# Left keys and values loaded with 16 positions outermost, and the last block's routing given in two parts

## The chip, the cores and the metric

The kernel runs on one core of a Trainium2 chip. The metric is the time of one launch on the device in microseconds; the time before is the median of three runs. The engines are TensorE (PE in the profile; its weight loads are PEld), VectorE (DVE), ScalarE (ACT), GpSimd (POOL) and SyncE (SP), which issues nearly all DMA transfers here.

## The reference

Three layers follow each other, all in float32.

```python
# attention: q, k, v are (8 batches, 8 heads, 576 positions, 64)
k_p = k.reshape(B, H, 72, 8, D).mean(axis=3)      # pooled keys: 72 per head
v_p = v.reshape(B, H, 72, 8, D).mean(axis=3)
attn = softmax(q @ k_p^T / 8)                      # with 1e-9 in the denominator
x = (attn @ v_p) -> (4608 tokens, 512)
# dense layer: w_in (512, 2048), w_out (2048, 512)
x = softplus(x @ w_in) @ w_out
# mixture of 8 experts: w1 (8, 512, 1024), w2 (8, 1024, 512)
logits = normalised(x) @ normalised(expert_emb)^T / tau
e = argmax(logits);  gate = softmax(logits)[e]
out = gate * (relu(x @ w1[e]) @ w2[e])
```

## The kernel before, in words

**Stages.** Tokens go in 12 blocks of 384 (`NB`). While TensorE computes the dense layer of one block (`mm1`, `mm2`, 16 feature chunks each), the attention of later tokens is worked in between, by a plan of gaps (`make_plan`). Each float32 product is made of three matmuls of split operands (`three`, lines 641 to 643), so every operand has a rounded part and a remainder: ScalarE copies the first, VectorE or GpSimd subtracts for the second. After a block's dense layer, `x2_out` splits its result and stores it to `x2s` in DRAM. `split_ss`, `logits_x`, `logits_s` and `route` then find the expert and the gate of each token. After the tenth block `pick` takes the most frequent expert so far; its weights are loaded and split (`load_a`, `make_a`, `load_w2`) during the last block, and behind it all tokens go through that expert in nine pairs of 512 tokens with a Strassen scheme: seven products (`mm3s`) and then `mm4s`. `load_b` fetches a pair's tokens, `make_t` forms four sums on GpSimd (eight instructions, line 923 to 934), `split_t` splits them on ScalarE and VectorE (942, 943) into the tile `T`, of which there is one buffer. `work_list` makes a list of the blocks that have tokens of other experts, which a loop at the end works off.

**Pooled keys and values.** For one batch the keys are 576 rows of 2 KB: 4 pairs of heads (`NJ`), and 144 pooled rows in a pair (`PK`), each row with its eight positions side by side. Of each pair 128 rows go the main way (`fetch_main`) and 16 are left (`LEFT`). `fetch_kl` loads the 64 left key rows into 64 partitions, pair by pair; `fetch_vl` loads the left value rows of two pairs into 32 partitions, three times over (rounded part, the same again, remainder), and this for two groups. `prep_k` and `prep_r` sum the eight positions, `kT` transposes the keys and puts the left columns behind the 128 of each pair, `build_r` masks the left values with `lm`, so that a matmul with `RV` picks a pair out of its group, `spread` copies the left weights of the attention three times side by side (line 364), `atrans` transposes them into `aR`, and `av` multiplies.

**What sets the order.** TensorE and SyncE work in the order in which the program calls them. For the first block the order of all engines is written out by hand (`ORDER`: a capital letter is a step of a generator, a small letter a load, H an idle matmul). After that a scheduler orders VectorE, ScalarE and GpSimd by the times of a simulation; an instruction given to `keep_in_program_order` is queued behind the instruction that its engine had been given last before it. The steps that follow a block's dense layer are put into a list, `front`, and one entry is taken per gap; in the part with the pairs `fronts(n)` takes n entries at fixed places:

```python
for p in range(1, NPR):
    run(split_t(p))
    fronts(2)
    if p + 1 < NPR:
        load_b(p + 1)
        run(make_t(p + 1))
    both(mm3s(p, 0), mm4s(p - 1, 1))
    fronts(1)
    both(mm3s(p, 1), mm4s(p, 0))
```

In the last block `make_t(0)` is taken step by step at chunks 4 to 11 and `split_t(0)` at chunks 12 to 15.

Of the kernel before, what the change touches and what calls it, by code (L numbers as in the profile page):

```python
# [20 lines left out]
def tile_attention_moe_moe(  # L21
# [77 lines left out]
    def setup_consts():  # L99
# [12 lines left out]
        nc.vector.tensor_scalar(pb, pi, LEFT, None, ALU.bitwise_and)  # L112
# [114 lines left out]
    def fetch_kl(b):  # L227
        st = stp.tile([P, POOL * D], F32, tag="st", name="st")
        nc.sync.dma_start(st[0:64, :], rows(k, b).rearrange("(j r) c -> j r c", j=NJ)[:, P:PK, :])
        st_t["kl", b] = st  # L230

    def fetch_vl(b, g):
        if b < 2:
            st = stp.tile([P, POOL * D], F32, tag="st", name="st")
        else:
            if g == 0:
                st_t["vl2", b] = stp.tile([P, 2, POOL * D], F32, tag="st", name="st")
            st = st_t["vl2", b][:, g, :]
        src = rows(v, b).rearrange("(j r) c -> j r c", j=NJ)[2 * g:2 * g + 2, P:PK, :]
        for i in range(3):  # L240
            nc.sync.dma_start(st[32 * i:32 * (i + 1), :], src)
        st_t["vl", b, g] = st
# [15 lines left out]
    def kT(b):  # L258
# [12 lines left out]
        copy(kb[:, :, P:PK], pk2.rearrange("p (j l) -> p j l", j=NJ))  # L271
# [28 lines left out]
    def build_r(b):  # L300
        vl = kv_t.pop(("l", b))
        vlm = kp.tile([96, NJ, D], F32, tag="vlm", name=f"vlm{b}")
        for jj in range(2):
            part = vlm.rearrange("p (g j) d -> p g j d", j=2)[:, :, jj, :]
            times(part, vl, lm[0:96, jj:jj + 1], b, "A" if alt(f"U{b}.m{jj}") else "G")
            yield
        nc.scalar.copy(RV[0:96, :, 1, :], vlm)
        yield
        nc.vector.tensor_tensor(RV[64:96, :, 1, :], vlm[64:96], f32(RV)[64:96, :, 1, :], ALU.subtract)
        yield  # L310
# [46 lines left out]
    def spread(t):  # L357
        e = e_t[t]
        el = qp.tile([P, 2, 3, 2, LEFT], F32, tag="el", name=f"el{t}")
        el_t[t] = el  # L360
        ev = e.rearrange("p (j h) k -> p j h k", h=2)
        for g in range(2):
            copy = nc.scalar.copy if alt(f"E{t}.e{g}") else nc.vector.tensor_copy
            copy(el[:, g], ev[:, 2 * g:2 * g + 2, 1, SP - LEFT:].unsqueeze(1).to_broadcast([P, 3, 2, LEFT]))
            yield
# [28 lines left out]
    def atrans(t):  # L394
# [8 lines left out]
        for g in range(2):  # L403
            nc.tensor.transpose(pl[:, g, :], el[:, g].rearrange("p r j l -> p (r j l)"), ident)
# [12 lines left out]
    def av(si, j):  # L417
# [9 lines left out]
        nc.tensor.matmul(pv[:, 0:n], rv, aR[:, j // 2, kk], start=False, stop=False)  # L427
# [95 lines left out]
    def emit_step(o):  # L523
# [14 lines left out]
        elif o[0] == "FV":  # L538
            for i in range(2):
                fetch_v(o[1], i)  # L540
            for i in range(2):
                fetch_vl(o[1], i)
# [195 lines left out]
    def route(blk):  # L738
# [8 lines left out]
        nc.gpsimd.tensor_tensor(n, lt[:, :, 2 * E], half, ALU.pow)  # L747
        nc.vector.tensor_scalar(n, n, 1e-6, taut, ALU.add, ALU.mult)
# [188 lines left out]
    def split_t(p):  # L937
# [3 lines left out]
        for i in (2, 0, 3, 1):  # L941
            nc.scalar.copy(t[:, 0, i], bf[:, i])
            nc.vector.tensor_tensor(t[:, 1, i], bf[:, i], f32(t)[:, 0, i], ALU.subtract)
# [180 lines left out]
    def loads(c, *a):  # L1124
# [10 lines left out]
        k0.0 k0.1 l0 q0 v0.0 q1 v0.1 i0 q2 r0.0 o0 l1 i1 H H H H H H H H H H H H K0 K0 H H H H H H H H K0 K0  # L1135
        H H K0 r0.1 Q0 K0 K0 H q3 H i2 Q0 B0 B0 H H B0 H V0 B0 V0 S0 S0 S0 Q1 S0 H q4 H S0 k1.0 Q1 H o1 o3 H
        k1.1 i3 H v1.1 v1.0 H i4 H o2 S0 V0 S1 V0 S0 S1 S1 S0 I0 W0 S1 S0 W0 S1 I0 S0 I0 Q2 S0 S1 W0 H H H
        I0 H H Q2 H H H H W0 E0 T0 I0 E0 S2 R0 S1 T0 T0 S2 S2 S1 I0 H H H H H O0 H S2 H I0 H H S1 S2 O0 O0
        I1 S2 O0 I1 R0 S2 I1 T0 T0 S2 Q3 O0 I1 H q5 H o4 Q3 H H H H S2 T0 H H H U0 U0 S2 S3 I2 i6 S1 o5 r1.0
        I2 I2 S3 S2 S3 U0 H I2 H H H H Q4 U0 S1 T2 E2 I2 Q4 E2 I2 I1 S3 T1 E1 E1 S3 T2 T2 S3 T1 I2 T1 T2 O1  # L1140
        T1 T1 K1 O1 O1 T1 S3 O1 T2 O3 O3 S3 O1 I1 T2 S3 O3 X2 I1 K1 O3 I3 X0 I3 I3 K1 O3 X2 I3 X1 X0 X2 K1
        X0 X3 - X1 K1 M0 X3 X1 r1.1 V1 i7 K1 X3 K1 M0 S3 I4 S3 M0 I4 M0 V1 I4 O2 B1 E3 E3 I4 B1 M1 G0 O2 B1
# [50 lines left out]
    with tc.block(schedule_with_timeline_sim=True), tc.manual_schedule(engines={mybir.EngineType.PE, mybir.EngineType.SP}):  # L1193
# [17 lines left out]
        def run_mm2(blk, fc):  # L1211
            run(mm2(blk, fc))
            if fc == NFC - 1:
# [6 lines left out]
                front.append(lambda: route(blk))  # L1220
                if blk == NB - 1:
# [113 lines left out]
```

## Time and profile before

| | |
|---|---|
| median of three runs | 1414.24 us (1412.03 to 1416.3) |
| profiled execution | 1414.68 us, span 1412.9 us |
| TensorE busy | 1364.6 us, 97% of the span, 8126 matmuls |
| VectorE busy | 901.1 us, 64% |
| ScalarE busy | 774.3 us, 55% |
| GpSimd busy | 419.5 us, 30% |
| granted TensorE clock | 0.988 of full speed in the mean |
| DMA | 100.00 MB, mean 71 GB/s |
| chain that ended last | PE 87%, DVE 6%, DMA 2%, ACT 2%, POOL 2%, issue 1% |

Busy time is time in which an instruction of the engine ran. An instruction of VectorE that waits for a memory port counts as running. The chain is followed back from the last instruction to what released each one. In a timeline, brackets behind an instruction give the idle time of its engine before it and what ended this.

### The profile page before, as it was taken

The page shows a single profiled execution, that of the slowest core. Times are in us where ns is not written, and L with a number is a line of the kernel's source. Part 1 is how long each engine was busy: PE and PEld are TensorE (multiplying, and loading weights), DVE is VectorE, ACT ScalarE, POOL GpSimd, SP SyncE. Part 2 cuts the span into 40 slices and gives each one's busy share as a digit, 9 for nine tenths or more (in the row PEclk, how much of TensorE's full clock was granted, in tenths as well). Part 3 has the DMA queues.
Part 4 walks back from the last instruction along what each step waited for, and adds up shares of the span by engine and source line. Part 5 has one row for each costly group of instructions (what it writes and reads, how often), then busy time and mean ns, then how long its engine had stood idle before and what let it go on. Part 6 is the DMA issues. An engine that isn't in the chain of part 4 may idle for free.

```text
span 1412.9 us, 21410 instructions
## 1 busy us (share of the span) xinstructions
PE 1364.6 (97%) x8126; PEld 1281.5 (91%) x8126; DVE 901.1 (64%) x1858; ACT 774.3 (55%) x1697; POOL 419.5 (30%) x374
## 2 busy tenths in 40 slices
PE   6789999999999999999999999999999999999998
PEld 5567889999999999999999999998988989989987
DVE  6989677677677676767676655567556444445332
ACT  4676656566676666667666767567632222223221
POOL 5843232223132231313223222164261222221200
PEclk8899999999999999999999999999999999999999
DMA  7562421212021210302120101042051302222000
GB/s 225 168 217 78 130 60 43 67 49 85 24 87 38 68 53 1 101 9 86 50 60 9 53 1 46 0 146 64 16 164 53 124 26 69 90 90 90 30 31 31
DMA packets 97881, 100.00 MB, mean 71 GB/s; under 512 B 40424, under 2 KB 79336, under 8 KB 97776
## 3 DMA queue, kind: packets, MB, share of 16 engines
q1 hardware_dynamic: 97776, 98.60, 22.5%
q8 instruction: 66, 1.08, 0.3%
q14 instruction: 39, 0.32, 0.1%
HBM read 70.27 MB, written 28.31 MB: 70 GB/s over the span
## 4 chain that ended last, share of the span: by engine, by line
PE 87%; DVE 6%; DMA 2%; ACT 2%; POOL 2%; issue 1%; SPq 0%; POOLq 0%; DVEq 0%; ACTq 0%
PE h L641 9%; PE h L643 9%; PE h L642 9%; PE acc L641 8%; PE acc L642 8%; PE acc L643 8%; PE y L641 4%; PE y L642 4%; PE y L643 4%; PE m L641 4%; PE m L642 4%; PE m L643 4%; PE pp L333 2%; PE acc L689 2%; DMA q<-in_q_dram 1%; PE lg L721 1%
## 5 line engine op out<-in xcount | busy, mean ns | idle before, releaser
L641 PE MATMUL h<-xT,wi 128*128 128x384 f32 x768 | 265.3, 345 | 3.6 <-DVE t L669 1.4
L642 PE MATMUL h<-xT,wi 128*128 128x384 f32 x768 | 257.9, 336 | 2.5 <-DVE xT L442 2.5
L643 PE MATMUL h<-xT,wi 128*128 128x384 f32 x768 | 258.3, 336 | 0.0
L641 PE MATMUL acc<-g,wo 128*128 128x384 f32 x704 | 241.0, 342 | 0.7 <-POOL wo L632 0.7
L642 PE MATMUL acc<-g,wo 128*128 128x384 f32 x704 | 236.4, 336 | 2.4 <-DVE g L673 2.4
L643 PE MATMUL acc<-g,wo 128*128 128x384 f32 x704 | 236.6, 336 | 0.0
L632 POOL TENSOR_TENSOR wo<-wof,wo 128x512 fp32r<-128x512 f32 x80 | 104.8, 1310 | 392.2 <-ACT wo L628 392.2
L657 ACT ACTIVATE t<-h 128x384 f32<-128x384 f32 x192 | 94.0, 490 | 154.0 <-PE h L643 152.5
L673 DVE TENSOR_TENSOR g<-t,g 128x384 fp32r<-128x384 f32 x176 | 142.2, 811 | 46.1 <-ACT g L671 46.1
L669 DVE SCALAR_TENSOR_TENSOR t<-h,t 128x384 f32<-128x384 f32 x176 | 97.0, 553 | 90.9 <-ACT t L661 88.9
L641 PEld LDWEIGHTS h<-xT,wi 128*128 128x128 f32 x768 | 145.0, 189 | 6.8 <-DVE t L669 2.0
L628 ACT CAST wo<-wof 128x512 fp32r<-128x512 f32 x176 | 109.3, 621 | 75.0 <-PE acc L643 73.5
L642 PEld LDWEIGHTS h<-xT,wi 128*128 128x128 f32 x768 | 144.8, 189 | 4.5 <-DVE xT L442 3.3
L643 PEld LDWEIGHTS h<-xT,wi 128*128 128x128 f32 x768 | 144.6, 188 | 0.0
L642 PEld LDWEIGHTS acc<-g,wo 128*128 128x128 f32 x704 | 132.9, 189 | 2.7 <-DVE g L673 2.7
L641 PEld LDWEIGHTS acc<-g,wo 128*128 128x128 f32 x704 | 132.7, 188 | 2.3 <-POOL wo L632 1.0
L643 PEld LDWEIGHTS acc<-g,wo 128*128 128x128 f32 x704 | 132.5, 188 | 0.0
L641 PE MATMUL y<-w2h,g 128*128 128x512 f32 x288 | 112.9, 392 | 0.0
L642 PE MATMUL y<-w2l,g 128*128 128x512 f32 x288 | 112.9, 392 | 0.0
L643 PE MATMUL y<-w2h,g 128*128 128x512 f32 x288 | 112.8, 392 | 0.0
L671 ACT CAST g<-t 128x384 fp32r<-128x384 f32 x176 | 89.6, 513 | 24.8 <-DVE t L669 24.0
L661 ACT ACTIVATE t<-t 128x384 f32<-128x384 f32 x192 | 100.7, 527 | 4.0
(223 smaller groups left out, 2856.4 us busy)
## 6 DMA issues: line engine op xcount, KB each, us to landing
x2s<-x SPq DMA_DIRECT2D x12, 1536.0 KB
b<-x2s SPq DMA_DIRECT2D x27, 512.0 KB
out_dram<-o SPq DMA_DIRECT2D x36, 256.0 KB
st<-in_k_dram SPq DMA_DIRECT2D x16, 512.0 KB
q<-in_q_dram SPq DMA_DIRECT2D x32, 256.0 KB
st<-in_v_dram SPq DMA_DIRECT2D x16, 512.0 KB
st<-in_moe_w_in_dram SPq DMA_DIRECT2D x16, 512.0 KB
st<-in_moe_w_out_dram SPq DMA_DIRECT2D x16, 512.0 KB
```

What stands on the lines that cost most here:

```text
L333: nc.tensor.matmul(pp[p0:p0 + n, i, :], qT[:, j, p0:p0 + n], kbd_t[b][:, j, :], start=True, stop=True)
L628: nc.scalar.copy(w[:, 0, :], wof[fc])
L632: eng.tensor_tensor(w[:, 1, :], wof[fc], f32(w)[:, 0, :], ALU.subtract)
L641: nc.tensor.matmul(ps, ll, rh, start=first, stop=False, skip_group_check=more)
L642: nc.tensor.matmul(ps, lh, rl, start=False, stop=False, skip_group_check=more)
L643: nc.tensor.matmul(ps, lh, rh, start=False, stop=last, skip_group_check=more)
L657: nc.scalar.activation(t, h, AF.Abs)
L661: nc.scalar.activation(t, t, AF.Ln, bias=1.0)
L669: nc.vector.scalar_tensor_tensor(t, h, 0.0, t, ALU.max, ALU.add)
L671: nc.scalar.copy(g[:, 0, :], t)
L673: nc.vector.tensor_tensor(g[:, 1, :], t, f32(g)[:, 0, :], ALU.subtract)
L689: nc.tensor.matmul(accs[blk][d], wof[fc][:, dd], f32(g)[:, 0, :], start=(fc == 0), stop=(fc == NFC - 1))
```

## The change

The left rows are loaded with the 16 positions outermost and the pairs inside, for keys and for values. All that depends on the order of the left rows follows: the columns of the transposed left keys, the mask `lm` (now by the lowest bit of the partition's number), the order in `spread`'s copies and the transposes, and which half of `aR` a pair uses. The left values of all four pairs come in one load per copy, three instead of six, into one tile; in `ORDER` the loads r0 and r1 stand for both groups, where r0.0 and r1.0 stood.

`route` gives control back after the power on GpSimd. For the last block alone it is taken in two parts, one entry of `front` later than before and the second part another entry later, with `work_list` behind it. In `split_t` both instructions of each split are kept in program order for the first pair.

```diff
--- before.py
+++ after.py
@@ -109,7 +109,7 @@
         nc.vector.tensor_scalar(hm[:, 0:1], pf, float(SP), None, ALU.is_lt)
         nc.vector.tensor_scalar(hm[:, 1:2], pf, float(SP), None, ALU.is_ge)
         pb = cp.tile([P, 1], I32, name="pb")
-        nc.vector.tensor_scalar(pb, pi, LEFT, None, ALU.bitwise_and)
+        nc.vector.tensor_scalar(pb, pi, 1, None, ALU.bitwise_and)
         nc.vector.tensor_copy(pf, pb)
         nc.vector.tensor_scalar(lm[:, 0:1], pf, 0.5, None, ALU.is_lt)
         nc.vector.tensor_scalar(lm[:, 1:2], pf, 0.5, None, ALU.is_ge)
@@ -226,20 +226,18 @@
 
     def fetch_kl(b):
         st = stp.tile([P, POOL * D], F32, tag="st", name="st")
-        nc.sync.dma_start(st[0:64, :], rows(k, b).rearrange("(j r) c -> j r c", j=NJ)[:, P:PK, :])
+        nc.sync.dma_start(st[0:64, :], rows(k, b).rearrange("(j r) c -> r j c", j=NJ)[P:PK])
         st_t["kl", b] = st
 
-    def fetch_vl(b, g):
-        if b < 2:
-            st = stp.tile([P, POOL * D], F32, tag="st", name="st")
-        else:
-            if g == 0:
-                st_t["vl2", b] = stp.tile([P, 2, POOL * D], F32, tag="st", name="st")
-            st = st_t["vl2", b][:, g, :]
-        src = rows(v, b).rearrange("(j r) c -> j r c", j=NJ)[2 * g:2 * g + 2, P:PK, :]
+
+
+    def fetch_vl(b):
+        st = stp.tile([P, 2, POOL * D], F32, tag="st", name="st")
+        src = rows(v, b).rearrange("(j r) c -> r j c", j=NJ)[P:PK]
         for i in range(3):
-            nc.sync.dma_start(st[32 * i:32 * (i + 1), :], src)
-        st_t["vl", b, g] = st
+            nc.sync.dma_start(st[32 * i:32 * (i + 1)], src)
+        for g in range(2):
+            st_t["vl", b, g] = st[:, g, :]
 
 
     def prep_k(b):
@@ -268,7 +266,7 @@
         (nc.scalar.copy if alt(f"B{b}.c1") else nc.vector.tensor_copy)(kb[:, :, 0:P], pk)
         yield
         copy = nc.scalar.copy if alt(f"B{b}.c2") else nc.vector.tensor_copy
-        copy(kb[:, :, P:PK], pk2.rearrange("p (j l) -> p j l", j=NJ))
+        copy(kb[:, :, P:PK], pk2.rearrange("p (l j) -> p j l", j=NJ))
         kbd_t[b] = kb
         yield
 
@@ -301,7 +299,7 @@
         vl = kv_t.pop(("l", b))
         vlm = kp.tile([96, NJ, D], F32, tag="vlm", name=f"vlm{b}")
         for jj in range(2):
-            part = vlm.rearrange("p (g j) d -> p g j d", j=2)[:, :, jj, :]
+            part = vlm.rearrange("p (j g) d -> p g j d", g=2)[:, :, jj, :]
             times(part, vl, lm[0:96, jj:jj + 1], b, "A" if alt(f"U{b}.m{jj}") else "G")
             yield
         nc.scalar.copy(RV[0:96, :, 1, :], vlm)
@@ -356,12 +354,12 @@
 
     def spread(t):
         e = e_t[t]
-        el = qp.tile([P, 2, 3, 2, LEFT], F32, tag="el", name=f"el{t}")
+        el = qp.tile([P, 2, 3, LEFT, 2], F32, tag="el", name=f"el{t}")
         el_t[t] = el
-        ev = e.rearrange("p (j h) k -> p j h k", h=2)
+        ev = e.rearrange("p (j g h) k -> p g h k j", g=2, h=2)
         for g in range(2):
             copy = nc.scalar.copy if alt(f"E{t}.e{g}") else nc.vector.tensor_copy
-            copy(el[:, g], ev[:, 2 * g:2 * g + 2, 1, SP - LEFT:].unsqueeze(1).to_broadcast([P, 3, 2, LEFT]))
+            copy(el[:, g], ev[:, g, 1, SP - LEFT:, :].unsqueeze(1).to_broadcast([P, 3, LEFT, 2]))
             yield
 
 
@@ -401,7 +399,7 @@
         e_t.pop(t)
         pl = ps_tile([96, 2, P], "pl")
         for g in range(2):
-            nc.tensor.transpose(pl[:, g, :], el[:, g].rearrange("p r j l -> p (r j l)"), ident)
+            nc.tensor.transpose(pl[:, g, :], el[:, g].rearrange("p r l j -> p (r l j)"), ident)
         yield
         for c0, d0, n in col_pieces(t):
             dd, cc = slice(d0, d0 + n), slice(c0, c0 + n)
@@ -424,7 +422,7 @@
         kk = slice(k0, k0 + n)
         nc.tensor.matmul(pv[:, 0:n], vl, aH[:, j, kk], start=True, stop=False)
         nc.tensor.matmul(pv[:, 0:n], vh, aL[:, j, kk], start=False, stop=False)
-        nc.tensor.matmul(pv[:, 0:n], rv, aR[:, j // 2, kk], start=False, stop=False)
+        nc.tensor.matmul(pv[:, 0:n], rv, aR[:, j % 2, kk], start=False, stop=False)
         nc.tensor.matmul(pv[:, 0:n], vh, aH[:, j, kk], start=False, stop=True)
         yield
         for c0, t0, m in pieces:
@@ -538,8 +536,7 @@
         elif o[0] == "FV":
             for i in range(2):
                 fetch_v(o[1], i)
-            for i in range(2):
-                fetch_vl(o[1], i)
+            fetch_vl(o[1])
         elif o[0] in ("PK", "KT", "PV", "PR"):
             if o not in preps:
                 preps[o] = {"PK": prep_k, "KT": kT, "PV": prep_v, "PR": prep_r}[o[0]](o[1])
@@ -745,6 +742,7 @@
         ts = slice(blk * TPB, (blk + 1) * TPB)
         n = sm.tile([P, TPB], F32, tag="n", name="n")
         nc.gpsimd.tensor_tensor(n, lt[:, :, 2 * E], half, ALU.pow)
+        yield
         nc.vector.tensor_scalar(n, n, 1e-6, taut, ALU.add, ALU.mult)
         nc.vector.reciprocal(n, n)
         z = sm.tile([P, TPB, E], F32, tag="z", name="z")
@@ -939,8 +937,12 @@
         t = p2[0].tile([P, 2, 4, 2, HT], F32R, tag="T", name=f"T{p}")
         t_t[p] = t
         for i in (2, 0, 3, 1):
-            nc.scalar.copy(t[:, 0, i], bf[:, i])
-            nc.vector.tensor_tensor(t[:, 1, i], bf[:, i], f32(t)[:, 0, i], ALU.subtract)
+            both_ins = [nc.scalar.copy(t[:, 0, i], bf[:, i])]
+            both_ins.append(nc.vector.tensor_tensor(t[:, 1, i], bf[:, i], f32(t)[:, 0, i], ALU.subtract))
+
+            if p == 0:
+                for ins in both_ins:
+                    tc.keep_in_program_order(ins)
             yield
 
     HOMES = ["g", "g", "g", "st", "W", "W", "wo", "wo"]
@@ -1132,14 +1134,14 @@
     }
 
     ORDER = """
-        k0.0 k0.1 l0 q0 v0.0 q1 v0.1 i0 q2 r0.0 o0 l1 i1 H H H H H H H H H H H H K0 K0 H H H H H H H H K0 K0
-        H H K0 r0.1 Q0 K0 K0 H q3 H i2 Q0 B0 B0 H H B0 H V0 B0 V0 S0 S0 S0 Q1 S0 H q4 H S0 k1.0 Q1 H o1 o3 H
+        k0.0 k0.1 l0 q0 v0.0 q1 v0.1 i0 q2 r0 o0 l1 i1 H H H H H H H H H H H H K0 K0 H H H H H H H H K0 K0
+        H H K0 Q0 K0 K0 H q3 H i2 Q0 B0 B0 H H B0 H V0 B0 V0 S0 S0 S0 Q1 S0 H q4 H S0 k1.0 Q1 H o1 o3 H
         k1.1 i3 H v1.1 v1.0 H i4 H o2 S0 V0 S1 V0 S0 S1 S1 S0 I0 W0 S1 S0 W0 S1 I0 S0 I0 Q2 S0 S1 W0 H H H
         I0 H H Q2 H H H H W0 E0 T0 I0 E0 S2 R0 S1 T0 T0 S2 S2 S1 I0 H H H H H O0 H S2 H I0 H H S1 S2 O0 O0
-        I1 S2 O0 I1 R0 S2 I1 T0 T0 S2 Q3 O0 I1 H q5 H o4 Q3 H H H H S2 T0 H H H U0 U0 S2 S3 I2 i6 S1 o5 r1.0
+        I1 S2 O0 I1 R0 S2 I1 T0 T0 S2 Q3 O0 I1 H q5 H o4 Q3 H H H H S2 T0 H H H U0 U0 S2 S3 I2 i6 S1 o5 r1
         I2 I2 S3 S2 S3 U0 H I2 H H H H Q4 U0 S1 T2 E2 I2 Q4 E2 I2 I1 S3 T1 E1 E1 S3 T2 T2 S3 T1 I2 T1 T2 O1
         T1 T1 K1 O1 O1 T1 S3 O1 T2 O3 O3 S3 O1 I1 T2 S3 O3 X2 I1 K1 O3 I3 X0 I3 I3 K1 O3 X2 I3 X1 X0 X2 K1
-        X0 X3 - X1 K1 M0 X3 X1 r1.1 V1 i7 K1 X3 K1 M0 S3 I4 S3 M0 I4 M0 V1 I4 O2 B1 E3 E3 I4 B1 M1 G0 O2 B1
+        X0 X3 - X1 K1 M0 X3 X1 V1 i7 K1 X3 K1 M0 S3 I4 S3 M0 I4 M0 V1 I4 O2 B1 E3 E3 I4 B1 M1 G0 O2 B1
         I4 G0 O2 B1 G0 O2 I3 T3 I4 G0 T3 G1 P0 O4 O2 O4 O4 O4 I6 P0 G1 I3 I4 G1 M2 I6 I6 O4 G1 O5 O5 O5 Z2
         I6 T3 I3 O5 P1 Z4 R1 G2 Z2 O5 o6 G2 P1 Z4 G2 o7 i5 q6 i9 i8 R1 I7 T3 M3 I7 G2 T3 I7 G2 T3 V1 o8 U1
         G2 U1 I7 M4 G3 O6 O6 O6 V1 I6 G3 O6 G3 P2 O7 O7 O7 I7 O6 G4 P2 I6 O7 I5 G4 G3 I5 S4 O7 G4 I5 Z6 S4
@@ -1217,8 +1219,13 @@
                 front.extend([lambda: None] * WAIT2)
                 front.append(lambda: [logits_x(blk, d) for d in range(KC)] + [logits_s(blk)])
                 front.append(lambda: None)
-                front.append(lambda: route(blk))
-                if blk == NB - 1:
+                r = route(blk)
+                if blk < NB - 1:
+                    front.append(lambda: run(r))
+                else:
+                    front.append(lambda: None)
+                    front.append(lambda: next(r))
+                    front.append(lambda: run(r))
                     front.append(work_list)
                 if blk == NB - 3:
                     front.append(count)
```

## Rows read from the trace of the kernel before

**Rows 1.** Stages of the run: length, busy time of each engine, granted clock, DMA share, GB/s.
```profile
0.00:110.00 110.00, 81.19 (x397) 65.40 (x398) 93.77 (x162) 66.89 (x132) 63.33 (x81) 0.88 0.64 196
110.00:300.00 190.00, 185.93 (x1075) 171.34 (x1075) 141.96 (x296) 120.29 (x266) 53.90 (x46) 1.00 0.26 74
300.00:900.00 600.00, 600.00 (x3624) 588.47 (x3623) 405.01 (x831) 398.72 (x875) 163.79 (x142) 1.00 0.16 47
...
1100.00:1380.00 280.00, 280.00 (x1759) 253.41 (x1759) 127.16 (x291) 77.62 (x186) 60.15 (x46) 1.00 0.19 65
```

**Rows 2.** Timeline of SyncE's DMA queue: start, time to issue, instruction (count).
```profile
14.78 4.55 SPq L241 DMA_DIRECT2D st<-in_v_dram  x3
19.43 0.53 SPq L173 DMA_DIRECT2D q<-in_q_dram  x1
```

**Rows 3.** Stages again: the first 10 us, and 22 to 24 us.
```profile
0.00:10.00 10.00, 5.54 (x29) 5.31 (x30) 4.22 (x14) 2.23 (x4) 4.81 (x19) 0.97 0.89 235
...
22.00:24.00 2.00, 0.04 (x1) 0.00 (x0) 2.00 (x5) 1.41 (x3) 1.29 (x1) 1.00 0.14 49
```

**Rows 4.** Timeline, 28 to 40 us: start, duration, instruction, [idle before it <- releaser].
```profile
29.67 1.08 PE L316 MATMUL pq<-ident,q 128*128 128x128 f32 x4 [7.62 <-DMA q<-in_q_dram]
...
28.98 0.72 POOL L193 TENSOR_TENSOR st<-st 96x256 f32<-96x256 f32 x1 [5.44 <-DMA st<-in_v_dram]
...
31.01 1.14 DVE L591 TENSOR_SCALAR st<-st 128x512 int32<-128x512 int32 x1 [2.63 <-DMA st<-in_moe_w_in_dram]
...
30.79 0.59 ACT L319 COPY qT<-pq 128x512 f32<-128x512 f32 x1 [4.43 <-PE pq L316]
...
32.60 1.14 POOL L353 TENSOR_TENSOR e<-e,sm 128x576 f32<-128x576 f32 x1
33.71 1.27 POOL L632 TENSOR_TENSOR wo<-wof,wo 128x512 fp32r<-128x512 f32 x1
34.94 1.15 POOL L353 TENSOR_TENSOR e<-e,sm 128x576 f32<-128x576 f32 x1
36.05 1.29 POOL L598 TENSOR_TENSOR st<-st,wi 128x512 f32<-128x512 f32 x1
...
33.91 3.97 DVE L593 SCALAR_TENSOR_TENSOR st<-st 128x512 int32<-128x512 int32 x1
...
39.13 0.25 DVE L364 COPY el<-e 128x96 f32<-128x96 f32 x1
```

**Rows 5.** Tile `st`, 0 to 130 us: durations in ns (min/median/max), first and last start.
```profile
L593 DVE SCALAR_TENSOR_TENSOR st<-st x16: 677/742/3970, 18.4 to 128.3; 128x512 int32<-128x512 int32 x16
```

**Rows 6.** Timeline, 957 to 963 us, VectorE and TensorE.
```profile
957.39 2.48 DVE L943 TENSOR_TENSOR T<-bf,T 128x512 fp32r<-128x512 f32 x4
...
962.08 0.69 PE L642 MATMUL acc<-g,wo 128*128 128x384 f32 x1 [2.45 <-DVE g L673]
```

**Rows 7.** Stages again: 960 to 970 us.
```profile
960.00:970.00 10.00, 7.92 (x38) 7.93 (x39) 5.90 (x8) 6.09 (x14) 6.99 (x5) 0.83 0.17 52
```

**Rows 8.** Timeline, 1052 to 1065 us, TensorE's waits and one of VectorE.
```profile
1052.20 0.37 PE L742 MATMUL pt<-ident,l 32*128 32x32 f32 x3 [1.12 <-ACT l L735]
...
1061.46 0.39 PE L641 MATMUL m<-T,a 128*128 128x256 f32 x1 [2.15 <-DVE c L1009]
...
1064.57 0.39 PE L641 MATMUL m<-T,a 128*128 128x256 f32 x1 [1.42 <-DVE c L994]
...
1058.48 1.24 DVE L748 TENSOR_SCALAR n<-n,taut 128x3 f32<-128x3 f32 x1 [1.19 <-POOL n L747]
```

**Rows 9.** Timeline, 1088 to 1136 us: SyncE's queue, GpSimd, VectorE.
```profile
1088.31 0.33 SPq L1083 DMA_DIRECT2D lst<-ebi  x1
...
1097.06 1.29 POOL L923 TENSOR_TENSOR bf<-bz 128x512 f32<-128x512 f32 x1 [33.25 <-DMA bz<-x2s]
...
1090.96 2.49 DVE L943 TENSOR_TENSOR T<-bf,T 128x512 fp32r<-128x512 f32 x4
...
1133.30 2.49 DVE L943 TENSOR_TENSOR T<-bf,T 128x512 fp32r<-128x512 f32 x4
```

## The prediction

> **What bounds the kernel now.** I read the stages first [rows 1]: from 300 to 900 us and from 1100 to 1380 us TensorE is busy for the whole stage, so nothing done on another engine there can shorten the run. What is open lies at the two ends of the table's gaps: in the first 110 us TensorE is idle for 110 - 81.19 = 28.8 us while VectorE works 93.77 of 110 us, and from 110 to 300 us it lacks 4.1 us. The stage between, 900 to 1100 us, I read by TensorE's own waits, and all those over 0.1 us from 957.1 to 1070 us are in [rows 6, 8]. The three parts of the change fall on three of these places, and because TensorE is full behind each of them, what is won there arrives at the end one for one. Time outside the span is 1414.68 - 1412.9 = 1.8 us and isn't touched. I make the sum against the profiled 1414.68 us, which is 0.44 us above the median of the runs, and take the saving from the median, 1414.24.
>
> **Part 1: left keys and values with 16 positions outermost.** Before, the source of a left key load has 4 outermost entries, that of a left value load 2; each batch has one load of 128 KB and six of 64 KB (two groups, three copies). After, both have 16, and the six are three of 128 KB. The same bytes move; SyncE issues three instructions less per batch.
>
> The cost of the old shape shows in the first block. SyncE's second triple of left value loads takes 4.55 us to issue, and the query load behind it is issued only at 19.43 us [rows 2]. While these drain, DMA is at 0.14 of its 16 engines, 49 GB/s, against 0.89 and 235 GB/s over the first 10 us [rows 3]: 0.14 of 16 is 2.2 engines, as many as the outermost size. Everything that was issued behind them ends late: TensorE waits 7.62 us for query tile 3 until 29.67, GpSimd 5.44 us for the left values until 28.98, VectorE 2.63 us for a weight tile until 31.01 [rows 4]. After, 5.37 MB stand in SyncE's order up to and with that query tile (sizes by the code); at the 235 GB/s of the first 10 us it lands at 22.9 us, and the left values before.
>
> Whether 16 outermost entries do spread over 16 engines no row shows. The Trainium skill, page "DMA: Bandwidth & Descriptors", section on why a DMA increments its semaphore by 16, says that a transfer runs on the largest number up to 16 that divides the slowest dimension of source and destination. By it the old loads had 4 and 2 engines and the new ones get 16; the 0.14 agrees for the 2.
>
> What is late next? Not the loads, but the engines' own order, written out by hand in this block. ScalarE has done its earlier work 4.43 us before it copies query tile 3 at 30.79, at 26.36, so this copy can follow there. VectorE is busy until its gap of 2.63 us begins, at 28.38; its last instructions before it are the reciprocals that GpSimd's first normalisation needs. From there GpSimd has, back to back, 1.15 + 1.27 + 1.15 + 1.29 = 4.86 us: it ends at 28.4 + 4.86 = 33.2 instead of 36.05 + 1.29 = 37.34 [rows 4]. VectorE's L593, 0.74 us in the median [rows 5], takes 3.97 us [rows 4] in that stretch and ends just after GpSimd's last one. If it is held so again, it ends about 4.1 us earlier than before; if not held, it comes after L591 and one maximum, at about 28.4 + 1.1 + 0.7 = 30.2, which is 7.7 us earlier. I take the first, since the same four instructions will stand beside it: **4.1 us**. The lower end is 0, if VectorE's work behind has slack that I don't see; up to 110 us it is busy nearly all the time, so the lead should hold.
>
> The Trainium skill's page "SBUF — State Buffer", section "SBUF: two separate sides", says that VectorE and GpSimd share a port pair as an exclusive lock for one whole instruction. By it L593 would lose one GpSimd instruction at most, 1.3 us, where the row shows three in succession; by the rule the saving is the 7.7 us case, by the row the 4.1 us one.
>
> Small edits. The copies of the left weights (L364) read two elements 288 apart where they read 16 in a row. VectorE's take 0.25 us [rows 4]. Twice that would be a bound above, zero one below; seven of them on VectorE in the first block make 0 to +1.7 us. I take 0: 96 elements in 0.25 us is mostly fixed cost. The mask, the transposes, the reordered copy of 64 key columns and the other index of aR have the same sizes as before: 0. In the later seven batches' loads the queue gains, but TensorE waits for no load after 110 us: 0.
>
> **Part 2: the splits of the first pair's sums held back.** They come from a scheduler that orders VectorE, ScalarE and GpSimd by a simulated time. It has put all four of `split_t(0)` at 957.39 us, 2.48 us of VectorE, ahead of the split of `wo` and of g, for which TensorE then waits 2.45 us until 962.08 [rows 6]; and in the 10 us around it the granted clock averages 0.83 [rows 7], which is 3.4 us at the lower level of 1.2 GHz. That costs 1.7 us if TensorE was busy through all of it; a part will lie in the wait itself, so I take 1.2 us. The program calls them one by one at the last four feature chunks of the block, well behind that place; each is now queued behind what its engine had been given by then. TensorE has no wait over 0.1 us between 962.08 and 1052.20 [rows 6, 8], so 2.48 / 4 = 0.6 us more per chunk on VectorE, and about as much on ScalarE, is hidden there; the sums are read only by the pair's products behind the last chunk. If that cover were gone, one split (0.6 us) would show. Saved: 2.45 + 1.2 = **3.65 us**, between 0 (the instruction it is pinned behind has itself been moved up) and 2.45 + 1.7 = 4.15.
>
> **Part 3: the last block's routing later, in two parts.** Now it follows `split_t(1)`. TensorE's transposes wait 1.12 us for ScalarE's copy of the logits; then VectorE, in order, stands 1.19 us at L748 for GpSimd's power, which is queued behind four sums of `make_t(2)`; behind L748 stand the sums of the products, and TensorE waits 2.15 and 1.42 us for them [rows 8]. After, nothing of the routing is there: 1.12 + 2.15 + 1.42 = **4.69 us** go. The first half comes at the place of the old work list, half a pair ahead, where GpSimd is idle (33.25 us until 1097.06) and the power waits for nothing. The second half and the work list come together half a pair later: the splits of two pairs stand 1133.30 - 1090.96 = 42.3 us apart, so 21 us [rows 9]. Three prices: the transposes and the work list's matmul are there before and after, 0; the routing's small VectorE instructions are the same as before and run in the gaps of the stage, 0, or at worst the 2.15 + 1.42 = 3.6 us that they cost now, if TensorE reaches the work list's matmul before they are done; I take 0, since they can start when the power is there, 21 us ahead. SyncE holds `load_b(3)` behind the list's store, which moves from 1088.31 to about 1109. GpSimd then starts its eight sums at 1097.06 + 21 = 1118 and needs 8 x 1.3 = 10.4 us, and VectorE splits them at 1133.30 [rows 9]: 4.9 us of slack, so 0, and a microsecond for each one by which the list is later than that.
>
> **Sum.** 4.1 + 3.65 + 4.69 = 12.4 us: 1414.2 - 12.4 = **1401.8 us**.
>
> **Rivals.**
> 1. The first block gains 7.7 instead of 4.1 us, since L593 gets in between GpSimd's instructions: 1398.2. For it: L591, beside GpSimd's instructions too, took 1.14 us and not 4; against it: the row at 33.91 [rows 4].
> 2. The transfers are hidden anyway: VectorE, with 93.77 of 110 us, sets the block's end, and what it gains by 41 us it loses in later port waits. Parts 2 and 3 alone, 8.3 us: 1405.9.
> 3. A new wait replaces the removed one: the second half of the routing lands behind the splits of `split_t(2)` on VectorE and TensorE waits at the work list's matmul. 12.4 - 3.6 = 8.8: 1405.4. It decides if VectorE gets the routing later than some 20 us after the power. Against it: the same scheduler took `split_t(0)` forward past many chunks of other work.
> 4. The pin does nothing, because what it is behind was itself moved up: 12.4 - 3.65: 1405.4.
> 5. Slower: the new load shapes change the scheduler's simulated time, so it reorders VectorE in blocks 1 to 11, and in each of the six later batches one stall like that at 962.08 appears, 3.65 us each: 22 us, 1414.2 - 12.4 + 21.9 = 1423.7. It decides from the fourth stall on (4 x 3.65 = 14.6 is more than 12.4). For it: the order isn't written down there. Against it: TensorE has had no idle time from 300 to 900 us under many such neighbours [rows 1].
>
> **Chances.** Forecast 0.50, rival 1 0.17, 2 0.14, 3 0.09, 4 0.05, 5 0.05. A difference under 0.3%, 4.2 us, can't be told from no change: the bounds are 1410.0 and 1418.5. All but rival 5 lie under 1410, but two of the smaller ones at once, or a stall or two of a new order, would end within; I give 0.85 faster, 0.10 same, 0.05 slower. The range: down to rival 1 with 2 us more (1396), up past rivals 2 to 4 with the el copies' 1.7 us and one small stall (1409).
>
> **What would show it.** Right: the query tile 3 transposes on TensorE near 22 us, not 29.67; the triple's issue below 3 us; L593 ending near 33.7; `T` splits on VectorE one at a time around 1000 us (an estimate), no 2.45 us wait for g; no wait of 1 us or more between 1045 and 1065; TensorE idle under 26 us in the first 110. Wrong: the DMA share still falls to 0.14 with a left load alone; TensorE waits at the work list's matmul; idle time between 300 and 900 us.

## The result and the profile after

The changed kernel takes 1400.37 us (median; 1398.62 to 1400.49), the kernel before beside it 1415.12 us: a ratio of 0.9899, 95% interval 0.9885 to 0.9913, 14.8 us saved where 12.4 were forecast. The profiled execution has 1400.3 us and a span of 1398.5. In a second timing (run e14 below) it took 1399.32 us, 0.9895 (0.9878 to 0.9911). Line numbers move by 2 or 3: L593, L591, L673, L943 and L994 of before are L590, L588, L670, L941 and L996.

Where the time came from is read first from the stages of the changed kernel, which answer to [rows 1]:

```profile
0.00:110.00 110.00, 86.94 (x425) 68.97 (x426) 97.66 (x173) 70.76 (x140) 67.67 (x84) 0.89 0.64 196
110.00:300.00 190.00, 185.95 (x1091) 173.33 (x1091) 141.45 (x297) 121.35 (x271) 56.20 (x49) 1.00 0.27 79
300.00:900.00 600.00, 600.00 (x3623) 588.47 (x3622) 404.78 (x841) 398.92 (x873) 160.36 (x138) 1.00 0.15 45
900.00:1100.00 200.00, 197.10 (x1206) 186.21 (x1205) 127.10 (x260) 106.21 (x230) 75.78 (x56) 1.00 0.24 78
```

The kernel before had, in the one stage that [rows 1] leave out:

```profile
900.00:1100.00 200.00, 190.68 (x1143) 180.41 (x1144) 125.99 (x264) 106.41 (x230) 78.36 (x59) 0.99 0.26 85
```

TensorE's idle time falls from 28.8 to 23.1 us in the first 110, and from 9.3 to 2.9 us between 900 and 1100; nothing is won from 110 to 300. From 300 to 900 it is full as before. A sharper measure needs a landmark: the first start of the logits' product (L721 before, L718 after) and its start in the block around 970 us, both read with the view of that one source line, and the span. A gain in the first block stands in the first column, one at the first pair's sums between the first two, one at the last block's routing between the last two. In brackets is the lead over the kernel before.

| kernel | first logits | logits near 970 | span | place 1 | place 2 | place 3 |
|---|---|---|---|---|---|---|
| before | 180.7 | 971.7 | 1412.9 | | | |
| changed | 173.4 (7.3) | 960.5 (11.2) | 1398.5 (14.4) | 7.3 | 3.9 | 3.2 |
| changed again (e14) | 171.7 (9.0) | 960.0 (11.7) | 1397.5 (15.4) | 9.0 | 2.7 | 3.7 |
| loads only (e1) | 171.4 (9.3) | 961.4 (10.3) | 1403.2 (9.7) | 9.3 | 1.0 | -0.6 |
| pin only (e2) | 181.7 (-1.0) | 970.0 (1.7) | 1412.0 (0.9) | -1.0 | 2.7 | -0.8 |
| routing only (e3) | 180.3 (0.4) | 971.5 (0.2) | 1408.9 (4.0) | 0.4 | -0.2 | 3.8 |
| forecast | | | | 4.1 | 3.65 | 4.69 |

Place 1 gave about twice its term (7.3 and 9.0 against 4.1); places 2 and 3 came out near theirs, place 3 about 1 us or more short.

**Place 1.** The timeline of SyncE's queue, TensorE, GpSimd and VectorE in the changed kernel (start, duration, instruction, idle before it), and the stage from 22 to 24 us, for [rows 2 to 4]:

```profile
8.66 2.66 SPq L238 DMA_DIRECT2D st<-in_v_dram  x3
...
13.62 0.37 SPq L173 DMA_DIRECT2D q<-in_q_dram  x1
...
21.30 0.63 PE L314 MATMUL pq<-ident,q 128*128 128x128 f32 x4 [1.24 <-DMA q<-in_q_dram]
...
21.52 0.73 POOL L193 TENSOR_TENSOR st<-st 96x256 f32<-96x256 f32 x1
...
26.91 1.15 POOL L351 TENSOR_TENSOR e<-e,sm 128x576 f32<-128x576 f32 x1 [0.70 <-DVE sm L348]
28.02 1.71 POOL L629 TENSOR_TENSOR wo<-wof,wo 128x512 fp32r<-128x512 f32 x1
29.69 1.32 POOL L351 TENSOR_TENSOR e<-e,sm 128x576 f32<-128x576 f32 x1
30.98 1.74 POOL L595 TENSOR_TENSOR st<-st,wi 128x512 f32<-128x512 f32 x1
...
26.47 0.27 DVE L348 RECIPROCAL sm<-sm 128x8 f32<-128x8 f32 x2
26.66 0.38 DVE L588 TENSOR_SCALAR st<-st 128x512 int32<-128x512 int32 x1
...
27.44 1.16 DVE L590 SCALAR_TENSOR_TENSOR st<-st 128x512 int32<-128x512 int32 x1
28.64 1.37 DVE L307 TENSOR_TENSOR RV<-vlm,RV 32x256 fp32r<-32x256 f32 x1
...
30.21 1.36 DVE L593 SCALAR_TENSOR_TENSOR st<-st 128x512 int32<-128x512 int32 x1
```

```profile
22.00:24.00 2.00, 0.91 (x9) 0.67 (x7) 2.00 (x5) 1.77 (x5) 1.84 (x4) 1.00 1.13 296
```

The DMA share between 22 and 24 us is 1.13 (this view's share can pass 1) where it was 0.14. Query tile 3 is issued 5.8 us earlier and is there at 21.3; GpSimd finds its left values waiting. VectorE's gap for the weight tile is gone: L588 follows at 26.66. And the instruction that took 3.97 us before takes 1.16 at 27.44, though the same four GpSimd instructions run back to back beside it: it ends 0.54 us after the first L351, and GpSimd's L629 takes 1.71 where [rows 4] have 1.27. The two engines take turns here. Before, VectorE was shut out to the end of the chain.

**Places 2 and 3.** The timeline with VectorE's first and last split of the first pair and TensorE's remaining waits ahead of them, and the stage around the old wait, for [rows 6, 7]; then the timeline of the last block: TensorE's two waits, VectorE's wait for GpSimd's power, the queue and GpSimd behind the list, and a VectorE row ahead of the last wait, for [rows 8, 9]:

```profile
987.12 0.69 DVE L941 TENSOR_TENSOR T<-bf,T 128x512 fp32r<-128x512 f32 x1
...
999.60 0.69 DVE L941 TENSOR_TENSOR T<-bf,T 128x512 fp32r<-128x512 f32 x1
...
942.43 0.44 PE L638 MATMUL h<-xT,wi 128*128 128x384 f32 x1 [0.38 <-DVE t L666]
949.97 0.44 PE L638 MATMUL h<-xT,wi 128*128 128x384 f32 x1 [1.00 <-DVE t L666]
```

```profile
960.00:970.00 10.00, 10.00 (x59) 9.04 (x58) 8.10 (x16) 6.77 (x15) 3.10 (x3) 1.00 0.02 4
```

```profile
1048.57 0.39 PE L638 MATMUL m<-T,a 128*128 128x256 f32 x1 [0.60 <-DVE c L996]
1113.82 0.39 PE L638 MATMUL m<-T,a 128*128 128x256 f32 x1 [0.58 <-DVE c L996]
...
1063.49 0.23 DVE L746 TENSOR_SCALAR n<-n,taut 128x3 f32<-128x3 f32 x1 [0.45 <-POOL n L744]
...
1093.66 0.33 SPq L1085 DMA_DIRECT2D lst<-ebi  x1
1094.09 0.61 SPq L912 DMA_DIRECT2D bz<-x2s  x1
...
1102.25 1.29 POOL L921 TENSOR_TENSOR bf<-bz 128x512 f32<-128x512 f32 x1 [38.79 <-DMA bz<-x2s]
...
1110.75 1.24 DVE L980 SCALAR_TENSOR_TENSOR g<-c,g 128x256 fp32r<-128x256 f32 x1
```

The 2.45 us wait for g and the dip of the clock are gone from 960 to 970. The routing's 4.69 us are gone, but GpSimd's sums of the next pairs now stand beside VectorE's gate products (L980 takes 1.24 us at 1110.75, and 0.41 where GpSimd is idle, as at 1090.72), and TensorE waits 0.60 and 0.58 us. The first is what stays of the 1.42 us of [rows 8], which stood at the same instruction; the second is new.

### The profile page after: what moved, and what is told of

It reads as the page before. It is cut to its first block, busy times and chain, and to the rows that moved or that the text cites. A ratio compares the mean times of both kernels' runs of the same rounds, so it can differ in the third digit from the quotient of the medians.

```text
span 1398.5 us, 21380 instructions
## 1 busy us (share of the span) xinstructions
PE 1361.6 (97%) x8126; PEld 1278.5 (91%) x8126; DVE 898.4 (64%) x1858; ACT 775.3 (55%) x1697; POOL 422.6 (30%) x374
## 4 chain that ended last, share of the span: by engine, by line
PE 89%; DVE 6%; ACT 2%; issue 1%; POOL 1%; DMA 1%; SPq 0%; DVEq 0%; POOLq 0%; ACTq 0%
PE h L640 9%; PE h L638 9%; PE h L639 9%; PE acc L638 8%; PE acc L640 8%; PE acc L639 8%; PE y L638 5%; PE y L639 5%; PE y L640 5%; PE m L638 4%; PE m L639 4%; PE m L640 4%; PE pp L331 2%; PE acc L686 2%; PE lg L718 1%
## 5 line engine op out<-in xcount | busy, mean ns | idle before, releaser
L629 POOL TENSOR_TENSOR wo<-wof,wo 128x512 fp32r<-128x512 f32 x80 | 105.3, 1316 | 392.1 <-ACT wo L625 392.1
L670 DVE TENSOR_TENSOR g<-t,g 128x384 fp32r<-128x384 f32 x176 | 141.1, 805 | 45.8 <-ACT g L668 45.8
```

Of the source, the lines that this page charges most:

```text
L629: eng.tensor_tensor(w[:, 1, :], wof[fc], f32(w)[:, 0, :], ALU.subtract)
L670: nc.vector.tensor_tensor(g[:, 1, :], t, f32(g)[:, 0, :], ALU.subtract)
```

## The experiments

**e1, e2, e3: each part alone.** The diffs are the three parts of the change (the pin of e2 is the program order kept for the first pair's splits).

> The kernel before with part 1 alone (left keys and values loaded with 16 positions outermost, three value loads of 128 KB, the order of the first block's loads that goes with them). Theory A, the three parts are independent and part 1 carries most: the lead at the logits' product after the first batch is 7.3 us in the changed kernel, so 1415.1 - 7.3 = 1407.8 us, with the first pair's wait of 2.45 us for g and the routing's 1.12, 2.15 and 1.42 us as before. Rival, the terms of the prediction's sum: 1415.1 - 4.1 = 1411.0. Rival, the three overlap (part of the lead is found again by the other two): the sum of the savings of the three single parts is clearly over or under 14.7 us.

> The kernel before with part 2 alone (splits of the first pair's sums kept in program order). Theory A: the lead of the changed kernel grows from 7.25 to 11.21 us over that place, so 1415.1 - 4.0 = 1411.1 us; the four splits stand one at a time near 1000 us and the 2.45 us wait for g is gone. Rival: the pin works only together with the new loads, since the scheduler's order came from the simulated time: no change, 1415.1. The first block of this kernel is the old one: if VectorE's L593 takes about 4 us beside GpSimd's four instructions again, the long row of the kernel before was no accident of one execution; if it takes about 1 us, it was.

> The kernel before with part 3 alone (the last block's routing and work list later, in two parts). Theory A, from the two traces: 4.69 us of waits go, 0.60 us comes at the features' product of the last block, 0.58 at that of the next pair and about 0.4 at the tail: 1415.1 - 3.2 = 1411.9 us. Rival, the new waits belong to the meeting of the parts and not to part 3: 1415.1 - 4.7 = 1410.4.

Measured: 1405.85 us (ratio 0.9941, 0.9927 to 0.9954), 1410.52 (0.9973, 0.9959 to 0.9987) and 1409.01 (0.996, 0.9946 to 0.9974). The prediction's 4.1 us for the loads falls: 9.0 by the runs and 9.3 at the landmark. The savings by the medians sum to 9.0 + 4.4 + 5.9 = 19.3 us against 14.8 for all three; with an uncertainty of some 1.9 us on each of the four numbers that is 3.9 on the difference, if they are independent, and the excess of 4.5 is a little over it. But the three single runs are measured against the same runs of the kernel before, so their errors partly go together, and by the table the parts nearly add: 9.3 + 2.7 + 3.8 = 15.8 against 14.4 and 15.4. Whether the medians show more than that is open. One overlap is seen in the rows of e1: the four splits still stand in a row, but the wait for g that they cause is 0.84 us and not 2.45, and another one ahead of it is longer. The -0.6 of e1 at place 3 goes with a dip of the clock: its stage from 1050 to 1060 us, behind the routing's wait, has a granted clock of 0.83, where the kernel before has 1.00 around its own. The -0.8 of e2 is a wait of 0.75 us at 1106.58 that the kernel before doesn't have.

```profile
949.53 2.49 DVE L940 TENSOR_TENSOR T<-bf,T 128x512 fp32r<-128x512 f32 x4
...
941.26 0.44 PE L638 MATMUL h<-xT,wi 128*128 128x384 f32 x1 [2.05 <-DVE t L666]
...
953.14 0.44 PE L639 MATMUL acc<-g,wo 128*128 128x384 f32 x1 [0.84 <-DVE g L670]
```

With the old loads, VectorE was shut out again. The rows are VectorE's long instruction and GpSimd's last one of the chain, first in e2, then in e3:

```profile
31.22 6.41 DVE L591 TENSOR_SCALAR st<-st 128x512 int32<-128x512 int32 x1 [2.68 <-DMA st<-in_moe_w_in_dram]
...
36.05 1.29 POOL L598 TENSOR_TENSOR st<-st,wi 128x512 f32<-128x512 f32 x1
```

```profile
29.96 6.44 DVE L591 TENSOR_SCALAR st<-st 128x512 int32<-128x512 int32 x1 [1.51 <-DMA st<-in_moe_w_in_dram]
...
34.82 1.30 POOL L598 TENSOR_TENSOR st<-st,wi 128x512 f32<-128x512 f32 x1
```

Both end 0.3 us after GpSimd's last (37.63 against 37.34, 36.40 against 36.12). So the long row of [rows 4] was no accident of one execution, though the instruction that is held differs (L593 there, L591 here).

What part 3 adds and leaves is seen in e3, at the two products where the changed kernel waits 0.60 and 0.58 us:

```profile
1059.40 0.39 PE L641 MATMUL m<-T,a 128*128 128x256 f32 x1 [0.59 <-DVE c L995]
...
1124.23 0.38 PE L641 MATMUL m<-T,a 128*128 128x256 f32 x1 [0.17 <-DVE c L995]
```

The first wait comes with part 3 alone, as theory A has it; most of the second doesn't, as the rival has it. By its interval the run saves 3.7 to 7.6 us, which leaves theory A's sum of 3.2 just outside, and the 3.8 of the table inside.

**e4: one group of loads, but 4 outermost.** Only the sources differ from the changed kernel:

```
-  rows(v, b).rearrange("(j r) c -> r j c", j=NJ)[P:PK]
+  rows(v, b).rearrange("(j r) c -> j r c", j=NJ)[:, P:PK, :]      (keys alike)
```

> The changed kernel, but the sources of the left keys' and values' loads have 4 outermost entries again and not 16; number, size and order of the loads stay as changed. The left rows come in another order than the rest of the kernel takes them, so the left positions' part of the result is computed from permuted rows; every instruction and size is the same. Theory A, the spread over DMA engines carries part 1: left loads run at 4 of 16 engines (a share near 0.25 while they stand alone), query tile 3 and the left values land later by some us, and the run takes 1403 to 1408 us. Rival, it is the fewer and earlier loads: no change from the changed kernel, 1400.4 within 1 us.

The rest of the kernel still takes the left rows with 16 outermost, so e4 leaves out the order that its loads would need; instructions and sizes are the same. Measured: 1402.35 us (0.991, 0.9895 to 0.9925), just under theory A's range, first logits at 174.5, a lead of 6.2.

**e11: 16 outermost, but two groups at the old places.** The counterpart:

```
-  r0 ... (one triple of 128 KB)
+  r0.0 ... r0.1 ahead of query tile 3 (two triples of 64 KB, [P:PK, g::2, :])
```

> The changed kernel, but each batch's left values come again in two groups of three 64 KB loads (16 positions outermost in each), with the second group at its old place ahead of query tile 3. Together with the run that has pairs first (4 outermost, one group: lead 6.2 us at the first logits where the same new loads gave 9.0 to 9.3 in three other runs, 7.3 in the changed kernel's own profile) this tells number and place of the loads from their spread. Theory S, it is the spread that ends them early: triples issued in under 3 us, query tile 3 on TensorE before 24 us, left values by 24, no VectorE instruction over 2 us there, 1399 to 1401.5 us. Theory O, it is the number and place of loads: query tile 3 and the left values late by 4 us or more, 1403 to 1407 us.

Measured: 1398.77 us (0.9886, 0.987 to 0.9903), just under theory S's range and far from theory O's, first logits at 170.8, a lead of 9.9. The stage from 22 to 24 us in e4, its timeline of VectorE, and the timeline of e11 with the second triple and query tile 3:

```profile
22.00:24.00 2.00, 0.00 (x0) 0.00 (x0) 2.00 (x5) 1.34 (x3) 1.82 (x2) 1.00 0.47 138
```

```profile
28.90 0.27 DVE L348 RECIPROCAL sm<-sm 128x8 f32<-128x8 f32 x2
...
30.50 1.78 DVE L590 SCALAR_TENSOR_TENSOR st<-st 128x512 int32<-128x512 int32 x1
```

```profile
13.54 2.77 SPq L240 DMA_DIRECT2D st<-in_v_dram  x3
...
21.41 0.63 PE L315 MATMUL pq<-ident,q 128*128 128x128 f32 x4 [1.37 <-DMA q<-in_q_dram]
```

The spread is the cause of the lead: number and place of the loads are worth nothing with 16 outermost (e11), and with 4 the DMA share of that stage lies between the two kernels (0.47; 0.14 before, 1.13 after) and so does the lead. In e4 VectorE takes turns with GpSimd already (1.78 us), but its reciprocals end at 29.1 and not at 26.7.

**e9, e10, e12: what shuts VectorE out?** In e9 all left values of the first batch are issued behind query tile 4, in e12 only GpSimd's half (on top of e11), in e10 the weight tile i2 is issued later:

```
e9   q2 [r0] o0 ... q4 +r0         e12  r0.0 ... q4 +r0.1
e10  q3 H [i2] Q0 ... k1.0 +i2
```

> The changed kernel with one edit in the order of loads: the first batch's left values are issued behind query tile 4, so GpSimd waits some 5 to 7 us for them (as before the change) and then has its sums and normalisations queued up; query tile 3 and VectorE's weight tile come as early as in the changed kernel. Theory A, a run of GpSimd instructions that had piled up behind a late load keeps VectorE out until it is through: a VectorE instruction of 3 to 6 us beside it, ending with GpSimd's last, and 1404 to 1407 us. Rival B, they alternate instruction by instruction as in the changed kernel (VectorE's of 1.2 to 1.8 us): 1400.4 plus only what GpSimd's own delay costs, 1401 to 1404 us.

> The changed kernel with the other edit in the order of loads: the expert weight tile i2 is issued some 7 us later, behind the second batch's first key load, so VectorE stands idle for it at L588 (as before the change) while GpSimd's sums and normalisations run on time. Theory C, it is a VectorE that comes out of an idle stretch while GpSimd is running back to back that is kept out: again a VectorE instruction of 3 to 6 us, ending with GpSimd's last one, and 1403 to 1407 us. Theory A of the run with late left values (the pile behind a late load is needed): VectorE's instructions take 1.2 to 1.8 us here; the run loses only the idle time, 1402 to 1404 us.

> As the run with groups apart, but the second group (GpSimd's half of the first batch's left values) is issued behind query tile 4; VectorE's half, its weight tile and query tile 3 come early. So GpSimd alone is late, and its sums and normalisations pile up behind the load; VectorE has no load to wait for. Theory A: VectorE is kept out until GpSimd's pile is through, one VectorE instruction of 3 us or more that ends with GpSimd's last one; 1402 to 1406 us. Rival B, they alternate, no VectorE instruction of that stretch over 2 us; 1400 to 1403 us.

Measured: e9 1405.24 us (0.9937, 0.9921 to 0.9954), e10 1398.24 (0.989, 0.9875 to 0.9905), e12 1399.85 (0.9894, 0.9878 to 0.9911). In e10 the tile was there in time: the row of L588 has no wait, so theory C was not put to the test, and only that the tile's place is worth nothing is learnt. Its row, then GpSimd's wait, its last instruction and VectorE's long one in e9, then the rows of e12:

```profile
27.86 0.38 DVE L588 TENSOR_SCALAR st<-st 128x512 int32<-128x512 int32 x1
```

```profile
25.07 0.72 POOL L193 TENSOR_TENSOR st<-st 96x256 f32<-96x256 f32 x1 [3.66 <-DMA st<-in_v_dram]
...
35.28 1.29 POOL L595 TENSOR_TENSOR st<-st,wi 128x512 f32<-128x512 f32 x1
...
32.12 4.74 DVE L588 TENSOR_SCALAR st<-st 128x512 int32<-128x512 int32 x1
```

```profile
24.83 1.07 POOL L193 TENSOR_TENSOR st<-st 96x256 f32<-96x256 f32 x1 [3.41 <-DMA st<-in_v_dram]
...
26.78 1.29 POOL L622 TENSOR_TENSOR wof<-wof,st 128x512 f32<-128x512 f32 x1
...
26.60 1.76 DVE L590 TENSOR_SCALAR st<-st 128x512 int32<-128x512 int32 x1
```

In e9 the hold is back with one edit in the order of the loads: 4.74 us, to 0.3 us after GpSimd's last (36.86 against 36.57), and VectorE had not stood idle just before it, which speaks against theory C. But e9 also stopped VectorE for 6.86 us at its own half of the left values, and the GpSimd instructions that held it did not stand right behind the load: GpSimd had done its sums and waited another 2.61 us, until 29.32, for ScalarE's e (L341). In e12 GpSimd is as late and its pile as long, and no VectorE instruction there takes more than 1.76 us; so a pile behind a late load isn't enough, and theory A as put down falls. What stands: every long hold (before, e2, e3, e9) is in a kernel in which the first batch's left values came late, and none is in the nine profiles in which they came early. What decides between taking turns and being shut out is open.

**e7, e8: the last block.** In e7 `load_b(p + 1)` is called ahead of `fronts(2)`; in e8 the entry `next(r)` is dropped.

> The changed kernel with the next pair's load of sums (load_b) called ahead of the two fronts, so that the last pair's load no longer stands on SyncE's queue behind the work list's store. Theory A, the load's delay is what part 3 lost at 1113.82: GpSimd's eight sums move from 1102-1113 back to where nothing of TensorE hangs on VectorE, the wait of 0.58 us at the features' product goes, and the run takes 1399.8 us (1400.4 - 0.6). Rival: the wait only moves, because the eight sums of GpSimd stand beside some VectorE work of the gate wherever they are: 1400.4, and a wait of about 0.6 at another place.

> The changed kernel with the last block's routing moved just as far but in one part (power and what follows it in one call, half a pair before the work list's matmul would otherwise be called). Theory A: the move alone takes the routing away from GpSimd's make_t(2), and the split is worth nothing, since the scheduler had put the second half right behind the first anyway (1062.6 and 1063.5): 1400.4 within 0.7. Rival, the split is what keeps VectorE from standing behind GpSimd's power: a wait of 1 us or more near the routing, 1401.5 to 1404.

Measured: 1400.87 us (0.9912, 0.9898 to 0.9926) and 1398.81 (0.989, 0.9876 to 0.9903). In e7 the rows are the rival's (the time lies within 0.5 us of it, and within 1.1 of theory A): GpSimd's sums now run from 1075.99 beside VectorE's work list, one of whose rows takes 1.30 us instead of 0.25, and TensorE waits 0.71 and 1.35 us there:

```profile
1084.19 1.30 DVE L1067 TENSOR_TENSOR wl<-wl 128x95 f32<-128x95 f32 x1
...
1085.88 0.38 PE L638 MATMUL m<-T,a 128*128 128x256 f32 x1 [0.71 <-DVE c L996]
1088.92 0.39 PE L638 MATMUL m<-T,a 128*128 128x256 f32 x1 [1.35 <-DVE c L1005]
```

In e8 no wait of the rival's kind is there, so theory A's mechanism holds, though 1398.8 lies 0.9 us under its range: the split of the routing is worth nothing, the move is all. VectorE waits 0.45 us for the power in both kernels, since the second half comes right behind the first anyway; in e8:

```profile
1062.59 0.23 DVE L746 TENSOR_SCALAR n<-n,taut 128x3 f32<-128x3 f32 x1 [0.45 <-POOL n L744]
```

**e13, e14: is any version better?** e13 has the edits of e8 and e10 together, e14 is the changed kernel once more.

> The changed kernel with both edits whose runs had the lowest medians: weight tile i2 issued later (1398.2) and the last block's routing in one part (1398.8). Theory: both are the changed kernel within what a measurement can tell, so this one too, 1398 to 1401 us, the interval of its ratio over that of the changed kernel. Rival, each is worth 1.5 to 2 us and they add: 1396.5.

> The changed kernel itself once more, beside the others on the same chip. Its first profile has a lead of 7.3 us at the first logits and a clock of 0.5 and 0.83 in the 10 us before 50 and 90 us; four other runs with the same loads had 9.0 to 9.3 there. Theory: those 2 us belong to the one execution and not to the kernel: median 1398.5 to 1400.5, and a profile whose lead at the first logits is 7 to 9.5. Rival: the changed kernel's own order costs them: lead again 7.3 and a dip near 85 us.

Measured: 1399.0 us (0.9883, 0.9867 to 0.99) and 1399.32 (0.9895, 0.9878 to 0.9911). Nothing adds up; e8, e10, e11, e13 and the changed kernel, at 1398.2 to 1400.4, can't be told apart, and none is shown to beat it. The 1.7 us between the two first landmarks belong to the execution: the first profile of the changed kernel has a granted clock of 0.58 from 84 to 88 us, 3.4 us of the 4 at the lower level of 1.2 GHz, which costs 1.7, and e14 has 1.00 there. The other profiles agree: e13 has such a dip too (0.83 from 80 to 90 us) and a lead of 7.7 us, while e1, e7, e8, e10 and e11 have 1.00 there and leads of 9.0 to 9.9. The stage of the changed kernel's first profile, then two stages and a row of the timeline of e14:

```profile
84.00:88.00 4.00, 3.85 (x7) 2.20 (x8) 2.30 (x5) 1.92 (x6) 0.84 (x1) 0.58 0.94 284
```

```profile
80.00:90.00 10.00, 8.35 (x44) 6.37 (x43) 7.37 (x16) 7.49 (x18) 3.79 (x3) 1.00 0.66 210
...
940.00:950.00 10.00, 8.47 (x39) 8.33 (x40) 7.70 (x12) 6.72 (x15) 4.83 (x4) 0.83 0.62 210
```

```profile
941.53 0.57 PE L638 MATMUL h<-xT,wi 128*128 128x384 f32 x1 [2.03 <-DVE t L666]
```

## Why the prediction was right, and where it was not

The direction, the three places and the rank of the views held; 1400.4 lies in the range, 1.4 us under the forecast. That it came so near is partly luck: part 1 gave 3.2 us more than its term in the first profile (4.9 in e14), and parts 2 and 3 together 1.2 us less (1.9).

- **Part 1: mis-sized, 4.1 against 7.3 to 9.9.** The step that failed is "I take the first, since the same four instructions will stand beside it". The same four stood there, and VectorE took turns with them. So rival 1 was the right mechanism. Its 7.7 us rested on reciprocals that end at 28.4; they end at 26.74, some 1.6 us earlier, and 7.7 + 1.6 = 9.3 is what e1 and (9.0) e14 show (L590 ends at 28.60, L593 of before at 37.88). Those 1.6 us the prediction didn't have: it let VectorE's work ahead of the gap stand where it was, but the spread loads speed that too. With 4 outermost (e4) VectorE takes turns and the reciprocals are late, and the lead is 6.2.
- The old row was read as a property of the four instructions, and beside the same four it need not come: VectorE loses one GpSimd instruction at a time in the changed kernel (27.44, 28.64, 30.21), and three to six in a row in before, e2, e3 and e9. The Trainium skill, page "SBUF — State Buffer", section "SBUF: two separate sides", has the port pair locked for one whole instruction; the first group of kernels agrees with that; in the second one instruction's lock is not enough to explain 3.97 to 6.44 us, and what gave GpSimd the pair several times running no run here shows.
- The spread, for which no row stood before, is shown by e11, which keeps number and place, and e4 fits: 2, 4 and 16 outermost in the left values' loads go with a share of 0.14, 0.47 and 1.13 in the stage from 22 to 24 us, where other loads run too.
- **Part 2: 3.65 against 3.9 and 2.7.** The wait went, and no cover failed. The clock was the uncertain term. TensorE's waits from 940 to 962 us before are 0.71, 0.38, 1.02 and the 2.45, in sum 4.56. In the first profile 0.86 (at 933.44) + 0.38 + 1.00 stay, so 2.3 of the 3.9 are waits, and the 1.6 that are left fit the dip, priced at up to 1.7. In e14 one wait of 2.03 us for t stays, which makes 2.5, and the dip doesn't go but stands at 940 to 950: nothing from the clock. The other profiles with the pin, read at the same two landmarks, bear this out: place 2 is 2.7 us in e2, e4, e8 and e14, which keep a dip of 0.83 in one 10 us stage there, and 3.7 to 4.2 in the changed kernel's first profile, e7 and e9 to e13, which have none. So the 1.2 taken for the clock was about right where the dip went, and it went in seven profiles of eleven. And 1.0 of the place's gain comes with the loads alone (e1).
- **Part 3: 4.69 against 3.2 and 3.7.** The routing's own waits went. But 0.60 of the 1.42 us stays, in e3 (0.59) too: GpSimd's sums of `make_t(2)` stand beside the same products whether the routing is there or not, and the prediction had given the whole wait to the routing. And `load_b(3)` behind the list's store was priced at 0 for its slack up to the splits. The splits were not late; but the eight sums, at 1102.25 in a kernel that is 15 us ahead by then (1117 in the times of before, where the prediction had 1118), now stand beside VectorE's gate products, at 0.58 (0.20 in e14). 4.69 - 0.60 - 0.58 = 3.5; some 0.2 more is lost behind TensorE's last matmul. e7 shows that the price goes along when GpSimd's sums are moved. In e8 the two parts of the change are worth no more than one.
- Rivals 2 to 5 did not come: TensorE has no wait at the work list's matmul, the pin worked alone, and from 300 to 900 us it has no idle time.

## What to carry to other kernels

Look at the outermost size of a small load before its bytes: a 64 KB load with 2 outermost entries held up everything behind it on the queue, and where its place in the order was kept, the spread alone gave the whole gain (e11). Where one profile shows an instruction several times its usual length beside another engine, don't carry the long or the short time into the changed kernel as the fixed price of those neighbours: keep both in the sum, for what precedes them decides. And a step that moves an engine's work to "where it is idle" is priced by who works beside it there, not only by its due time.

## Hardware that was not expected

- VectorE was shut out by a back-to-back chain of GpSimd for 3.97, 6.41, 6.44 and 4.74 us in four kernels, and took turns with the same instructions (1.16 to 1.78 us) in the others. The condition stays open; it was not tried to give GpSimd a pile without any load.
- Some 3.4 us at the lower clock (1.7 us lost) stand at different places in two executions of the changed kernel: at 84 to 88 us in one, right behind a wait of TensorE of 1.30 us, at 940 to 950 in the other, around its wait of 2.03. But e14 has the same wait at 84 us (1.29) and as much idle time from 80 to 90 us with the clock at 1.00. A single profile of this kernel can't size a term below 2 us.
